# A spectral filter's transfers in 16-run pieces, and three loads begun later

## The chip, the cores and the metric

The kernel runs on one core of one Trainium2 chip. The metric is the time of one execution on the device in microseconds; several runs are given by their median. TensorE is called PE, VectorE DVE, ScalarE ACT, GpSimd POOL and SyncE SP. SP starts nearly all the transfers. The core has 16 DMA engines, which share all of them.

## The reference

Two blocks with residuals are computed forward and backward in bfloat16 over x of shape (1, 2048, 448): a spectral filter A and a token MLP B. The outputs are the result and the gradients to x, the filter's two parts, w1, b1, w2 and b2.

```python
def _A_ref(x, w_r, w_i):                      # x (1, 2048, 448); w_r, w_i (2048, 225)
    X = rfft2(x.astype(float32))
    X = X * (w_r + 1j * w_i)
    return irfft2(X, s=(S, D)).astype(bfloat16)

def _B_ref(x, w1, b1, w2, b2):                # w1 (2048, 1792), w2 (1792, 2048)
    h = layernorm(x)
    u = gelu(einsum("bsd,sf->bdf", h, w1) + b1)
    return (einsum("bdf,fs->bds", u, w2) + b2).transpose(0, 2, 1)

x = A_x
h  = x + _A_ref(layernorm(x), A_w_r, A_w_i)
h2 = h + _B_ref(layernorm(h), B_w1, B_b1, B_w2, B_b2)
# outputs: h2, and the vector-Jacobian product with grad_out for x, w_r, w_i, w1, b1, w2, b2
```

## The kernel before

The two-dimensional transform is done in steps of matmuls. `row_a` and `row_b` transform 16 row groups (the 448 axis and the first part of the 2048 axis), and after every second group a transfer on SP (line 667) puts the result into the buffer `D2` in another order of partitions, the D2 reshape. `s2_stage` then runs over four sets of groups: for each it does the second part of the 2048 axis with small matmuls on `D2` (line 223), multiplies with the filter (`fwd_mult` or `bwd_mult`), turns the product back with small matmuls, and sends it by SP (line 696) to the buffer `D3`, the D3 reshape. `inv_rows` does the inverse rows. Between these steps `fill(n)` gives PE n matmuls of an independent product from a list of pending generators: in the forward pass w2's product with grad_out (`dg_gen`, whose tiles `load_w2T` brings in by DMA transposes, line 306), in the backward pass the weight gradients out_6 and out_4 (`gw_gen`, operands by the transposes of lines 1166 and 1180, stores on lines 1275 and 1272).

PE, SP, DVE and ACT run their instructions in the order in which the kernel writes them, each engine in its own order; semaphores join them. A DMA is started by an instruction in SP's order, so an instruction of SP that takes long, or waits, keeps back all that was written after it. `defer` writes a transfer a little later, by an estimated PE clock. Matmuls go through line 218, DVE and ACT instructions through line 82.

The filter is kept in `W`, a view of region `rW`. `w_io` moves it between DRAM and `rW`: six moves for w_r and six for w_i, of which the generator gives one at each `next`. It loads w_r and w_i in the forward pass (row step t of the loop takes `W_AT[t]` moves) and stores their gradients, out_2 and out_3, in the tail (`gx_consumer` at step t takes as many moves as t occurs in `GW_AT`). The issue is line 572 in both cases. Of the six moves, the first brings the positive half of the frequencies: 64 rows of 7200 contiguous bytes, in DRAM as 4 x 16 rows. The four that follow bring the mirrored half, each 16 partitions in runs of 450 bytes (DF = 225 elements), and the last one 16 rows.

In the backward pass `load_du(q)` (line 1166) transposes a quarter of du for the second weight gradient, and `load_xall(q)` (line 1185) loads a quarter of x into region `rE` for the last LayerNorm's gradient. Quarter 3 of du is loaded in the du loop; quarters 0 and 2 inside `s2_stage`, which calls `after[s]()` when set s has been multiplied; quarter 1 in the last row steps, as are quarters 0 and 1 of x. Quarters 2 and 3 of x are loaded in the tail (`X_AT`).

In the tail, `gx_consumer` works on 8 slots of `r448`, and every second step stores two of them to out_1 (line 1340); eight steps later a slot is written again by DVE.

Of the kernel before, what the change touches and what calls it, by code (L numbers as in the profile page):

```python
# [17 lines left out]
P = 128  # L18
S = 2048
D = 448  # L20
DF = 225
# [18 lines left out]
N_FILL_B = (16, 16, 30, 8, 24, 8)  # L40
# [61 lines left out]
class Ring:  # L102
# [7 lines left out]
    def next(self):  # L110
        v = self.views[self.i % len(self.views)]
        self.i += 1
        Ring.release(v)
        return v
# [8 lines left out]
def kernel(  # L123
# [47 lines left out]
    def ring(reg, off, count, *dims):  # L171
        n = int(np.prod(dims))
        return Ring([cut(reg, off + i * n, *dims) for i in range(count)])

    def ps_ff(parts=P):
        return psum.tile([P, 512], F32, tag="ff", bufs=4, name="ps_ff")
# [5 lines left out]
    def evac(out, in_, scale=None):  # L182
        n = int(np.prod(in_.shape[1:]))
        if load[0] + sc.cost('copy', n, False) <= load[1] + ve.cost('tensor_copy', n, in_.dtype == BF16):
            if scale is None:
                sc.copy(out=out, in_=in_)
            else:
                sc.activation(out=out, in_=in_, func=ACT.Copy, scale=scale)
        elif scale is None:
            ve.tensor_copy(out=out, in_=in_)  # L190
        else:
            ve.tensor_scalar(out=out, in0=in_, scalar1=scale, scalar2=None, op0=ALU.mult)
# [5 lines left out]
    def run_due():  # L198
        while later and later[0][0] <= clock[0]:
            later.pop(0)[2]()  # L200

    def defer(us, fn, *views):
        state = [fn]

        def run():
            if state:
                state.pop()()
        later.append((clock[0] + us, len(later), run))
        later.sort(key=lambda x: x[0])
        for v in views:  # L210
            Ring.held.setdefault(id(v), []).append(run)

    def flush():
        while later:
            later.pop(0)[2]()
# [6 lines left out]
    def small(out, lhsT, rhs, start, stop):  # L222
        nc.tensor.matmul(out, lhsT=lhsT, rhs=rhs, start=start, stop=stop)  # L223
        clock[0] += int(np.prod(rhs.shape[1:])) / 38400.0

    def blk(i):
        return slice(32 * i, 32 * i + 32)
# [4 lines left out]
    def set_groups(s):  # L232
        return [8 * (s // 2) + s % 2 + 2 * a for a in range(4)]
# [154 lines left out]
    def newton_gp(v, y, sl):  # L388
        vi, yi = nt_i[:, 0, sl], y.bitcast(I32)
        a = nt_f[:, 0, sl]  # L390
        gp_.tensor_scalar(out=v, in0=v, scalar1=LN_EPS, scalar2=None, op0=ALU.add)
        gp_.tensor_scalar(out=yi, in0=v.bitcast(I32), scalar1=-0.5, scalar2=RSQRT_MAGIC, op0=ALU.mult, op1=ALU.add)
        for c0, c1 in RSQRT_STEPS:
            gp_.tensor_tensor(out=a, in0=y, in1=y, op=ALU.mult)
            gp_.tensor_tensor(out=a, in0=a, in1=v, op=ALU.mult)
            gp_.tensor_scalar(out=a, in0=a, scalar1=c0, scalar2=c1, op0=ALU.mult, op1=ALU.add)
            gp_.tensor_tensor(out=y, in0=a, in1=y, op=ALU.mult)
# [163 lines left out]
    def w_io(dr, di, store):  # L561
        Wq = Wc.rearrange("(q s) c g k -> s q c g k", s=2)
        for c_, d in ((0, dr), (1, di)):
            moves = [(Wq[0][:, c_].rearrange("q g k -> q (g k)"), 0, [[16 * DF, 4], [P * DF, 16], [1, 16 * DF]])]
            for i in range(4):
                g0 = 0 if i else 1
                moves.append((Wq[1][16 * i:16 * i + 16, c_, g0:NG, :], P - 16 * i - g0,
                              [[P * DF, 16], [-DF, NG - g0], [1, DF]]))
            moves.append((Wq[1][0:16, c_, 0, :], 64, [[P * DF, 16], [1, DF]]))
            for sb, row, dims in moves:  # L570
                d_ap = bass.AP(d.tensor, d.offset + row * DF, dims)
                nc.sync.dma_start(out=d_ap if store else sb, in_=sb if store else d_ap)  # L572
                yield
# [3 lines left out]
    X_ring = ring(rC, 0, 2, 4, 2, KW)  # L577
# [10 lines left out]
    def rowbase(s_):  # L588
        return 32 * (s_ // 4) + s_ % 4
# [80 lines left out]
    def s2_stage(get_x, on_mult, n1, n2, gap, after=None, scale=None):  # L670
        flush()

        def four(tables, s, turn, rhs):
            gs = set_groups(s)
            ps = [ps_ff()[:, 0:452].rearrange("p (c k) -> p c k", c=2) for _ in gs]
            for t, c, start, stop in ((tables[0], None, True, False), (tables[1], 0, False, False), (tables[2], 1, False, True)):
                for a, g in enumerate(gs):
                    for r in range(4):
                        x, o = rhs(a, g, r), ps[a][blk(r + turn * a & 3)]
                        small(o if c is None else o[:, c, :], lhsT=t[blk(r), g, :], rhs=x if c is None else x[:, 1 - c, :],  # L680
                              start=start, stop=stop)
            run_due()
            return ps

        y = None
        for s in range(5):
            if s < 4:
                x = get_x(s)
                for a, pv in enumerate(four((Vt, Ut, Un), s, 1, lambda a, g, r: D2[blk(r), g])):
                    evac(out=x[:, a], in_=pv, scale=scale)  # L690
            fill(n1)
            if s:
                for g, pv in zip(set_groups(s - 1), four((VTt, UTt, UTn), s - 1, -1, lambda a, g, r: y[blk(r), a])):
                    ab = r452_ring.next()
                    evac(out=ab, in_=pv)
                    defer(RESH_LAG, lambda g=g, ab=ab: resh[0].dma_start(out=D3[rowbase(g):rowbase(g) + 29:4, :, :, :], in_=ab), ab)
            if s < 4:
                y = Y_ring.next()
                for j in range(2):
                    on_mult(s, j, x[:, 2 * j:2 * j + 2], y[:, 2 * j:2 * j + 2])  # L700
            if after is not None and s in after:
                after[s]()
            fill(n2)
        fill(gap)
# [52 lines left out]
    def fill(n):  # L757
        while n > 0 and pending:
            try:
                next(pending[0])  # L760
                n -= 1
                if row_ops:
                    row_ops.pop(0)()
            except StopIteration:
                pending.pop(0)
# [75 lines left out]
    ve.reciprocal(out=rstd_x[:, 2:4], in_=rstd_x[:, 2:4])  # L841
    Rs.update({t: scale_R(t) for t in range(2, 4)})
    w_loads = w_io(A_w_r, A_w_i, False)
    uv = gen_UV()
    gen_inv_cols(0)
# [10 lines left out]
    GROUPS = {0: (6, 8), 1: (8, 10), 3: (10, 12), 5: (12, 14), 7: (14, 16)}  # L856
    STATS = {0: (6, 7), 1: (8, 9), **{t: (t + 8,) for t in range(2, 8)}}
    INV_S = {10: 0, 11: 1, 12: 2, 13: 3}
    W_AT = {t: 1 for t in range(1, 13)}
    for c in range(2):  # L860
        for e in range(2):
            sc.copy(out=Rp.rearrange("p (e a q b c) -> p c e a q b", e=2, c=2, q=8, a=2)[:, c, e],
# [3 lines left out]
    for t in range(NT):  # L866
# [21 lines left out]
        if t in GROUPS:  # L888
            a, b = GROUPS[t]
            newton_gp(mvx[:, a:b, 1], rstd_x[:, a:b], slice(a, b))  # L890
        for _ in range(W_AT.get(t, 0)):
            next(w_loads, None)
# [271 lines left out]
    def load_du(q):  # L1164
        n = du_t[q].shape[1] * 512
        nc.sync.dma_start_transpose(out=du_t[q].rearrange("p j b q -> p (j b) q"), in_=rD[:, 2048 * q:2048 * q + n])
# [10 lines left out]
    def st_load(n):  # L1177
        if n < 15:
            reg, j = order[n]
            nc.sync.dma_start_transpose(out=st_at[n], in_=reg[:, j * 1024 + 64:j * 1024 + 960])  # L1180
# [3 lines left out]
    def load_xall(q):  # L1184
        nc.sync.dma_start(out=xall[:, 4 * q:4 * q + 4, :], in_=x_pt[:, 4 * q:4 * q + 4, :])

    def rows(t):
        if t < NT:
            row_a(t, Rm[:])
            fill(2)  # L1190
        row_b(t - 4, True)
        fill(2 if t < NT else 1)
# [86 lines left out]
    for t in range(NT - LAG, NT + 4):  # L1279
        if t == 13:  # L1280
            st_load(3)
        if t == 14:
            load_xall(0)
        if t == 15:
            load_du(1)
        if t == 16:
            load_xall(1)
        if t == NT - 2:
            fill(8)
        rows(t)  # L1290
    fill(N_FILL_B[2])
    Meter.slack = 7.0
    s2_stage(lambda s: X_ring.next(), bwd_mult, 14, 22, N_FILL_B[4], {1: lambda: load_du(0), 3: lambda: load_du(2)},
             2.0 * INV_SD)
    Meter.slack = 2.0
    g_out = w_io(out_2, out_3, True)
    X_AT = {0: 2, 4: 3}
    GW_AT = tuple(range(12))

    def gx_consumer(t, py):  # L1300
        if t in X_AT:
            load_xall(X_AT[t])
        for _ in range(GW_AT.count(t)):
            next(g_out, None)
# [87 lines left out]
```

## Time and profile before

| | |
|---|---|
| Median of 3 runs | 370.64 us (367.15, 370.64, 371.81) |
| Profiled execution | 368.16 us, of which span 366.3 us |
| PE, DVE, ACT, POOL busy | 332.6, 251.1, 196.6, 64.0 us |
| DMA, mean over the span | 213 GB/s, 78.02 MB |
| Mean granted PE clock | 0.973 |

The span runs from the first to the last recorded instruction of one execution; the execution's own time is longer by what lies around it. Lines such as L572 are lines of the kernel. A row of a timeline gives start, length, engine, line, operation, output and inputs, count, and in brackets the idle time ahead of it with its releaser. SPq is SP's queue of DMA issues: its length is how long the issue held SP, not how long the data took. A row of windows gives, for each stretch, its length, the busy time of PE, PEld, DVE, ACT and POOL, then PE's granted clock, the mean busy share of the DMA engines and GB/s. The share can pass 1.00, because a packet's time is booked where its record stands and packets overlap.

### The profile page before, as it was taken

The numbers are of one execution on the slowest core, as the hardware profiler recorded it, in microseconds if no ns is written. First come the engines' busy times: TensorE is split into PE (matmuls) and PEld (weight loads), VectorE is DVE, ScalarE is ACT, GpSimd is POOL, SyncE is SP. The second block draws the span as 40 slices with busy tenths as digits, with TensorE's granted clock in tenths as the row PEclk, the third lists the DMA queues.
The fourth block names the chain that finished last, engine by engine and source line by source line (L and its number), as shares of the span: only waits on it lengthen the run. The fifth ranks groups of instructions, "written<-read, shape, count | busy, mean of one in ns | idle before, by whom it ended". The sixth has DMA issues, their size and how long they took to land.

```text
span 366.3 us, 7779 instructions
## 1 busy us (share of the span) xinstructions
PE 332.6 (91%) x2810; PEld 174.2 (48%) x2819; DVE 251.1 (69%) x666; ACT 196.6 (54%) x431; POOL 64.0 (17%) x219
## 2 busy tenths in 40 slices
PE   8679907989999999999999999999799999999694
PEld 3346604445654555555555555545333434555351
DVE  8896415781494788768224888786479984599594
ACT  5457512544696653622421345565368775679563
POOL 5766000000122000001000111110000000157361
PEclk9989977999999999999999999999999999999988
DMA  8999889767994999788776889839959699999784
GB/s 211 283 174 162 175 181 240 162 123 193 315 253 206 295 347 246 169 214 255 186 190 157 190 165 176 161 88 224 319 175 259 188 233 256 277 161 242 190 309 168
DMA packets 147006, 78.02 MB, mean 213 GB/s; under 512 B 95448, under 2 KB 139736, under 8 KB 146840
## 3 DMA queue, kind: packets, MB, share of 16 engines
q1 hardware_dynamic: 146680, 77.13, 85.6%
q8 instruction: 22, 0.36, 0.4%
q10 hardware_dynamic: 288, 0.39, 0.3%
q14 instruction: 16, 0.13, 0.1%
HBM read 25.71 MB, written 22.04 MB: 130 GB/s over the span
## 4 chain that ended last, share of the span: by engine, by line
PE 70%; DVE 9%; SPq 6%; DMA 6%; ACT 4%; issue 3%; POOL 0%; DVEq 0%; ACTq 0%
PE ps_mm L218 59%; PE ps_ff L218 7%; DVE r L82 5%; SPq L306 3%; PE ps_ff L223 3%; DVE rS L82 3%; DMA out_dram<-r 3%; ACT rO L82 2%; DMA rE<-in_A_x_dram 1%; DMA rA<-in_A_x_dram 1%; DVE rA L82 1%; SPq L667 1%; SPq L572 1%; DMA r<-rX 1%; SPq L316 1%
## 5 line engine op out<-in xcount | busy, mean ns | idle before, releaser
L218 PEld LDWEIGHTS <-r 128*128 128x128 bf16 (+2 forms) x600 | 56.3, 105 | 48.3 <-issue 5.7
L218 PEld LDWEIGHTS <-rS 128*128 128x128 bf16 (+2 forms) x496 | 40.3, 98 | 39.5 <-issue 6.6
L218 PE MATMUL ps_mm<-rD,r 128*128 128x448 bf16 x224 | 44.5, 352 | 0.0
L82 ACT CAST rO<-ps_mm 128x512 bf16<-128x512 f32 (+1 forms) x66 | 35.4, 583 | 14.5 <-PE ps_mm L218 10.4
L218 PEld LDWEIGHTS <-rst 128*128 128x128 bf16 (+1 forms) x320 | 23.6, 97 | 31.3 <-issue 14.4
L218 PE MATMUL ps_mm<-rC,rE 128*128 128x448 bf16 x144 | 33.1, 367 | 2.0 <-DMA rC<-in_grad_out_dram 1.9
L218 PE MATMUL ps_mm<-rB,r 128*128 128x448 bf16 x160 | 31.2, 352 | 0.1
L218 PE MATMUL ps_mm<-r,rst 128*128 128x512 bf16 (+2 forms) x144 | 28.1, 354 | 0.0
L218 PE MATMUL ps_mm<-rG,rst 128*128 128x512 bf16 (+1 forms) x122 | 26.7, 380 | 0.5 <-issue 0.3
L82 ACT CAST r<-ps_ff 128x452 bf16<-128x452 f32 x41 | 22.6, 588 | 8.3 <-PE ps_ff L223 6.0
L82 DVE SCALAR_TENSOR_TENSOR r<-ps_mm,b2col,r 128x448 bf16<-128x448 f32 x16 | 10.9, 683 | 19.9 <-PE ps_mm L218 17.0
L82 ACT ACTIVATE r<-ps_mm,rstd_h 128x448 bf16<-128x448 f32 x16 | 10.1, 633 | 26.8 <-PE ps_mm L218 26.8
L82 ACT ACTIVATE r<-rC 128x448 bf16<-128x448 bf16 x16 | 9.1, 571 | 26.6 <-DMA out_dram<-r 18.9
L218 PE MATMUL ps_mm<-rE,rS 128*128 128x448 bf16 x112 | 21.5, 352 | 0.0
L82 ACT ACTIVATE rG<-rG 128x896 bf16<-128x896 bf16 x14 | 13.3, 950 | 14.9 <-DVE rG L82 14.7
L218 PEld LDWEIGHTS <-rO 128*128 128x128 bf16 (+1 forms) x165 | 15.2, 98 | 12.3 <-ACT rO L82 0.2
L82 ACT CAST rS<-ps_ff 128x512 bf16<-128x512 f32 x31 | 17.9, 580 | 5.3 <-PE ps_ff L218 5.1
L82 ACT CAST rG<-ps_mm 128x512 bf16<-128x512 f32 (+1 forms) x33 | 16.5, 544 | 6.6 <-PE ps_mm L218 6.4
L218 PEld LDWEIGHTS <-rE 128*128 128x128 bf16 x144 | 13.8, 101 | 13.0 <-issue 4.0
L218 PE MATMUL ps_ff<-csI,rAT 113*128 113x224 bf16 (+1 forms) x108 | 19.4, 303 | 0.6 <-ACT rAT L82 0.4
L82 ACT CAST rAT<-ps_ff 113x512 bf16<-113x512 f32 x24 | 14.0, 591 | 10.7 <-PE ps_ff L218 10.6
L1134 POOL TENSOR_SCALAR lcol<-lcol 128x1 f32<-128x1 f32 x16 | 8.3, 519 | 64.9 <-ACT r L82 64.9
(189 smaller groups left out, 598.5 us busy)
## 6 DMA issues: line engine op xcount, KB each, us to landing
out_dram<-rO SPq DMA_DIRECT2D x34, 256.0 KB
r<-in_B_w_dram SPq DMA_DIRECT2D x5, 1024.0 KB
r<-r SPq DMA_DIRECT2D x32, 113.0 KB
rS<-in_B_w_dram SPq DMA_DIRECT2D x4, 896.0 KB
r<-r SPq DMA_DIRECT2D x12, 226.0 KB
out_dram<-rG SPq DMA_DIRECT2D x10, 256.0 KB
rO<-in_B_w_dram SPq DMA_DIRECT2D x2, 1024.0 KB
rC<-in_grad_out_dram SPq DMA_DIRECT2D x4, 448.0 KB
```

The costliest lines, as they stand in the source:

```text
L82: fn(**kw)
L218: nc.tensor.matmul(out, lhsT=lhsT, rhs=rhs, start=start, stop=stop)
L223: nc.tensor.matmul(out, lhsT=lhsT, rhs=rhs, start=start, stop=stop)
L306: nc.sync.dma_start_transpose(out=wT, in_=B_w2[j * P:(j + 1) * P, :].rearrange("f (t c) -> f t c", c=P))
L316: nc.sync.dma_start(out=go_tp[:, 4 * q:4 * q + 4, :], in_=go_tp_d[:, 4 * q:4 * q + 4, :])
L572: nc.sync.dma_start(out=d_ap if store else sb, in_=sb if store else d_ap)
L667: defer(RESH_LAG, lambda: resh[0].dma_start(out=D2[u:u + 125:4, 8 * e:8 * e + 8].rearrange("p g c k -> p (g c k)"), in_=cs.rearrange("p x ...
L1134: gp_.tensor_scalar(out=m1, in0=ms, scalar1=-1.0 / D, scalar2=None, op0=ALU.mult)
```

## The change

The filter's positive half is moved in four transfers of 16 rows instead of one of 64; each stands ahead of one of the four mirrored moves. So `w_io` gives 9 moves instead of 6 for each part. `W_AT` and `GW_AT` take two moves in odd steps, so that all 18 are still written by step 12 of the row loop, or step 11 of the tail. In the backward pass three transfers move out of the row steps into `s2_stage`: du's quarter 1 to after set 0, x's quarter 0 to after set 1 (behind du's quarter 0, which was there), and x's quarter 1 to after set 2.

```diff
     def w_io(dr, di, store):
         Wq = Wc.rearrange("(q s) c g k -> s q c g k", s=2)
         for c_, d in ((0, dr), (1, di)):
-            moves = [(Wq[0][:, c_].rearrange("q g k -> q (g k)"), 0, [[16 * DF, 4], [P * DF, 16], [1, 16 * DF]])]
+            moves = []
             for i in range(4):
+                moves.append((Wq[0][16 * i:16 * i + 16, c_].rearrange("l g k -> l (g k)"), 16 * i, [[P * DF, 16], [1, 16 * DF]]))
                 g0 = 0 if i else 1
                 moves.append((Wq[1][16 * i:16 * i + 16, c_, g0:NG, :], P - 16 * i - g0,
                               [[P * DF, 16], [-DF, NG - g0], [1, DF]]))
...
-    W_AT = {t: 1 for t in range(1, 13)}
+    W_AT = {t: 2 if t % 2 else 1 for t in range(1, 13)}
...
     for t in range(NT - LAG, NT + 4):
         if t == 13:
             st_load(3)
-        if t == 14:
-            load_xall(0)
-        if t == 15:
-            load_du(1)
-        if t == 16:
-            load_xall(1)
         if t == NT - 2:
             fill(8)
         rows(t)
     fill(N_FILL_B[2])
     Meter.slack = 7.0
-    s2_stage(lambda s: X_ring.next(), bwd_mult, 14, 22, N_FILL_B[4], {1: lambda: load_du(0), 3: lambda: load_du(2)},
+    s2_stage(lambda s: X_ring.next(), bwd_mult, 14, 22, N_FILL_B[4], {0: lambda: load_du(1), 1: lambda: (load_du(0), load_xall(0)), 2: lambda: load_xall(1), 3: lambda: load_du(2)},
              2.0 * INV_SD)
...
-    GW_AT = tuple(range(12))
+    GW_AT = tuple(range(12)) + tuple(range(1, 12, 2))
```

## Prediction

> **What bounds the kernel now.** I read the page first. TensorE (PE) is busy 91% of the span, so a gain can come only out of the places where PE stands.
>
> ```profile
> PE 332.6 (91%) x2810; PEld 174.2 (48%) x2819; DVE 251.1 (69%) x666; ACT 196.6 (54%) x431; POOL 64.0 (17%) x219
> ```
>
> PE's timeline has three gaps of more than a microsecond in the stretches that the change touches: 10.76 us before 57.11, 1.89 us before 260.59 and 3.27 us before 345.82. The bracket at the end of a row is the idle time and its releaser.
>
> ```profile
> 57.11 0.82 PE L223 MATMUL ps_ff<-r,Vt 32*32 32x452 bf16 x16 [10.76 <-DMA r<-rX]
> 260.59 0.41 PE L223 MATMUL ps_ff<-r,Vt 32*32 32x452 bf16 x16 [1.89 <-issue]
> 345.82 0.38 PE L218 MATMUL ps_ff<-RTm,r 128*113 128x128 bf16 x4 [3.27 <-DVE r L82]
> ```
>
> **Gap one** (forward). PE waits for the D2 reshape of rows 12 and 13 (L667). The rows were evacuated by 44.4, but their reshape is issued at 54.69. SyncE's timeline (SP; columns: start, length, line) says why: from 22.39 to 55.9 it issues back to back.
>
> ```profile
> 22.39 0.73 SPq L572 DMA_DIRECT2D rW<-in_A_w_r_dram  x1
> 23.16 7.10 SPq L306 DMA_TRANSPOSE rO<-in_B_w_dram  x1
> 30.31 0.71 SPq L572 DMA_DIRECT2D rW<-in_A_w_r_dram  x1
> 31.14 2.89 SPq L306 DMA_TRANSPOSE rE<-in_B_w_dram  x1
> ...
> 41.23 1.29 SPq L572 DMA_DIRECT2D rW<-in_A_w_i_dram  x2
> 42.62 6.59 SPq L306 DMA_TRANSPOSE rE<-in_B_w_dram  x1
> ```
>
> Four transposes of one size: two hold SP 2.89 and 3.07 us (the latter at 36.79, left out), two hold it 7.10 and 6.59. The two long ones stand behind the 64-run load of w_r and of w_i. The windows view gives the DMA rate (last column, GB/s) behind those loads, and behind the same two transfers as stores in the tail, beside an ordinary stretch each (30 to 42, 327 to 337):
>
> ```profile
> 24.00:30.00 6.00, 6.00 (x45) 3.95 (x44) 5.89 (x23) 4.42 (x10) 3.97 (x16) 0.86 0.94 93
> 30.00:42.00 12.00, 12.00 (x215) 8.06 (x214) 6.11 (x21) 7.91 (x16) 3.96 (x18) 1.00 1.02 187
> 320.00:326.00 6.00, 6.00 (x45) 2.98 (x44) 5.91 (x18) 4.47 (x12) 2.70 (x9) 1.00 1.05 113
> 327.00:337.00 10.00, 10.00 (x77) 5.67 (x74) 9.64 (x31) 9.02 (x26) 7.13 (x18) 1.00 1.10 284
> ```
>
> 93 and 113 GB/s where other transfers reach 187 and 284: the 64-run transfer runs on few DMA engines, and what is queued behind it waits.
>
> The Trainium skill, "DMA: Bandwidth & Descriptors", section "Why a DMA increments its semaphore by 16 and not by 1", says how many engines a copy gets: the largest number up to 16 that divides the slowest dimension of both sides. By it the old form (64 partitions against a DRAM pattern that begins with 4) gets 4 engines, the new one (16 against 16) gets 16. No row of before shows a 16-run copy of 7200 bytes, so that half of the rule is open.
>
> **Gap two** (start of the backward filter stage). Here too PE waits for a D2 reshape. SP's timeline before it holds the moved work:
>
> ```profile
> 248.43 0.52 SPq L1185 DMA_DIRECT2D rE<-in_A_x_dram  x1
> 249.04 0.54 SPq L667 DMA_DIRECT2D r<-r  x1
> 249.64 3.33 SPq L1166 DMA_TRANSPOSE rC<-rD  x1
> 253.01 1.05 SPq L1275 DMA_DIRECT2D out_dram<-rO  x2
> 254.17 0.39 SPq L1185 DMA_DIRECT2D rE<-in_A_x_dram  x1
> 254.61 1.63 SPq L667 DMA_DIRECT2D r<-r  x2
> ```
>
> **Gap three** (tail). The chain of waits shows an out_1 store that takes 9.86 us to land, issued right behind the 64-run store of w_i's gradient (333.96); VectorE (DVE) needs its buffer.
>
> ```profile
> 334.67 9.86 DMA out_dram<-r
> ...
> 344.65 1.13 DVE r L82 x3
> ```
>
> **The change, part by part.**
>
> *Forward loads.* Removed: the hold behind two 64-run loads. Against the mean of 2.89 and 3.07 (2.98) that is 7.10 - 2.98 + 6.59 - 2.98 = 7.73 us of SP time. Added: six issues on L572 (18 instead of 12). One took a median 0.607 us, the 64-run form 0.62 (at 315.52) like the 256-run forms, so I keep 0.61 plus a gap of 0.05: 6 x 0.66 = 3.96 us. All stand on SP ahead of the reshape that PE waits for, so both count in full: -7.73 + 3.96 = **-3.8 us**. The other steps do not get in the way: the ring slots of the transposes were free long before (the third weight tile's last matmul ran near 32 us), and the last rows were ready at 44.4, so SP stays the bound until 9.7 us are gained. Bounds: if the new runs' bytes are still paid by SP at the 229 GB/s of 49 to 55 us, each group holds 460.8 KB / 229 = 2.0 us and the gain is gone (-7.73 + 4.0 + 3.96 = +0.2). If a 16-run copy issues like the cheapest 128-run ones (0.39 at L1185), eight of them save 0.2 each, and with a hold 0.6 shorter the gain is 6.0. I take 3.8, because the transposes of 2.89 and 3.07 themselves stand right behind 112.5 KB transfers of L572, nearly the new size.
>
> A rule speaks against it. The row: on SP, transfers of 112.5 KB follow one another every 0.66 us, and from 49 to 55 us a queue of such pieces moves 229 GB/s. The Trainium skill, same page, "Bandwidth" and "Rules for kernel authors", wants 1 MiB per DMA and says that splitting over partitions only serializes; its SWDGE fit is 2.0 us plus bytes over 436 GB/s. By that, as an estimate, one copy of 460.8 KB is 3.1 us and four are 9.1, so the change would cost 6 us a group.
>
> *Moved loads.* x quarter 0 (0.52), the transpose of du's second quarter (3.33) and x quarter 1 (0.39) leave SP's queue ahead of the reshape: 4.24 us of issue and 0.92 MB of x. PE had other work until 258.70, and the evacuation that SP waited for (253.30) stays. Then the reshape goes out near 254.3; with the 2.28 us that the forward one took from issue to landing and 1.5 us for the 0.5 MB of stores ahead of it (about 340 GB/s around it) it lands at 258.1, before PE is free. **-1.9 us**, the whole gap; at least 1.0 if 0.9 of it stays. At their new place these three come after set 0, 1 and 2 of s2_stage. What queues behind them on SP: output stores of out_6 (L1275), weight tiles for later matmuls (L1180), and D3 reshapes (L696), needed at 312. The rO buffers of the stores are the tightest: six, one filled every 1.9 us, so 11.4 us round; less the 1.5 us of deferral and some 3.5 us to land, SP may be 6.4 us late before an evacuation stops. The transpose brings 1.8 to 3.3 (the four calls of L1166). Cost nothing, with that cover. The moved data is needed at 300.85 (rC) and at 317 (rE): some 35 us early.
>
> *Tail stores.* Again six issues more, but SP is not what the tail waits for: the 64-run stores held it (2.32 and 4.37 us at 318 and 320, where 0.6 and 1.5 are usual). The out_1 store of row 3 must land within 5.57 us (334.67 to 340.24). Less a hold of 3.6 to 4.1, 9.86 becomes 5.8 to 6.3, still 0.2 to 0.7 late; the store before (329.75) landed within 6.04 without stopping DVE, and a reshape lands in 2.28. From 340.24 DVE loses 4.42 us; PE loses 3.27 plus some 1.7 at the clock of 0.50 that the windows show from 347 to 350. Both are busy to the end after it, DVE being the tighter. **-4.4 us**, bounds 3.7 and 5.0.
>
> **Sum**: -3.8 - 1.9 - 4.4 = -10.1 us. PE works without a gap of more than a microsecond from 113 to 259, and loads there are released by its progress, so the first gain is carried. The profiled execution took 368.16 us (span 366.3 and 1.9 around it): 358.1. The median of three runs, 370.64, stands 2.5 above it, the lowest run 1.0 below; I go half way up: **359.3 us**.
>
> **The rivals.**
> - *The split only adds issues; it does not do what it says.* The waits view puts 3.8 us of the long transposes down to PE (L545), not to DMA; if the transposes were long by themselves, SP is 3.96 us later at gap one, gap three stays and gap two goes: 368.16 + 3.96 - 1.9 = 370.2, slower than before. It decides from where the relief per transpose is under 1.98 us. Against it: PE passed that tile's slot 10 us before, and both long ones stand behind the same form. 6%.
> - *The tail store is late anyway*, because ordinary stores fill the queues (284 GB/s from 327 to 337): 368.16 - 5.7 = 362.5. Against it: between 337 and 342 hardly half of that moved. 13%.
> - *The moved transfers hold the filter stage*: transpose 3.3 and x 0.92 MB at 340 GB/s, 2.7, make the out_6 stores over 6.4 us late and evacuations wait, as one did for 1.4 us near 257. 358.1 + 6.0 = 364.1. For it: SP issued back to back from 247 to 266. Against it: it stood idle later in set 0. 10%.
>
> **How the numbers follow.** Forecast 71%. Its bounds give gains from 4.5 (0.2 lost, 1.0, 3.7) to 12.9 (6.0, 1.9, 5.0), so 355.3 to 363.7 on the profiled time, 366.1 on the median: range 355 to 366, which takes in the second and third rival. A measurement of this kernel tells about 2% from no change; below 363.2 us it is faster by more. That holds for most of the forecast (0.68), about half of the second rival (0.07) and a corner of the third: 0.77. Within 2%: 0.18. Slower by over 2% needs the first rival with the tail's issues on the path: 0.05.
>
> **What would show it.** Right: all L306 transposes between 22 and 45 us near 3 us, with no stretch near 100 GB/s behind the L572 loads; PE's first gap near 7 us; no gap before the backward L223 group; no out_1 store over 6 us on the chain and no DVE wait on out_dram. Wrong: transposes of 6 us and more behind the new loads, a wait of ACT or DVE on out_dram<-rO within s2_stage, or a new PE gap there.

## The result and the profile after

The changed kernel takes 358.27 us, the median of four runs (357.57 to 359.34), against 370.6 us before: a ratio of 0.9684, 95% interval 0.9615 to 0.9754. Faster by 3.2%, 1 us under the forecast of 359.3. The profiled execution took 358.56 us, span 356.8. Ratios leave out executions more than 1.5% above the fastest of their kernel: eleven of the 25 of the kernel before (median 370.77 us) that stand beside the first four experiments, and in two experiments the profiled one (431 and 856 us), which the medians given for these two leave out too.

The page's line of busy time; PE's work is what it was, the span is 9.5 us shorter:

```profile
PE 331.0 (93%) x2810; PEld 173.6 (49%) x2819; DVE 251.1 (70%) x666; ACT 196.6 (55%) x431; POOL 63.6 (18%) x219
```

PE's timeline of the changed kernel at the three places of the forecast. The first gap is 6.89 us instead of 10.76; the other two rows have no bracket, so PE did not stand there at all:

```profile
53.49 0.82 PE L223 MATMUL ps_ff<-r,Vt 32*32 32x452 bf16 x16 [6.89 <-DMA r<-rX]
255.27 0.41 PE L223 MATMUL ps_ff<-r,Vt 32*32 32x452 bf16 x16
337.06 0.39 PE L218 MATMUL ps_ff<-RTm,r 128*113 128x128 bf16 x4
```

How far one and the same piece of PE's work moved shows where the time came from. A row_a group (before at 247.13, after at 243.77) starts 3.4 us earlier: the forward part. The gw_gen group at 272.70 is now at 267.38, 5.3 us earlier: another 2.0 from the start of the filter stage. The last matmuls (358.22, now 347.84) are 10.4 us earlier: another 5.1 in the tail. The span gained 9.5; what follows the last matmuls took 0.9 us more.

SP's timeline (start, length, line) where the two long transposes were; line numbers shift with the edits, 572 is 573 here:

```profile
22.73 1.37 SPq L573 DMA_DIRECT2D rW<-in_A_w_r_dram  x2
24.14 3.68 SPq L306 DMA_TRANSPOSE rO<-in_B_w_dram  x1
...
39.71 1.89 SPq L573 DMA_DIRECT2D rW<-in_A_w_i_dram  x3
41.70 2.52 SPq L306 DMA_TRANSPOSE rE<-in_B_w_dram  x1
```

7.10 and 6.59 us became 3.68 and 2.52, 7.5 us together; the filter's issues on SP are more by six. Windows rows (last column GB/s) behind the loads and, in the tail, in the stretch of the gradients' stores:

```profile
24.00:28.00 4.00, 3.99 (x26) 2.59 (x26) 3.97 (x17) 3.01 (x8) 2.18 (x11) 0.75 1.00 120
316.00:322.00 6.00, 6.00 (x51) 3.74 (x48) 5.94 (x20) 4.77 (x13) 3.58 (x11) 1.00 0.95 231
```

The tail's 113 GB/s became 231. Behind w_r's loads the rate rose only from 93 to 120, so the sign "no stretch near 100 GB/s" is met in part at best: there the shorter hold of the transpose tells the change, not the rate. And SP's queue ahead of the backward filter stage, without the moved transfers: the second of the two reshapes in the last row is the one that PE waited for before.

```profile
245.07 0.54 SPq L668 DMA_DIRECT2D r<-r  x1
245.70 1.04 SPq L1276 DMA_DIRECT2D out_dram<-rO  x2
246.84 2.13 SPq L668 DMA_DIRECT2D r<-r  x2
```

### The profile page after: what moved, and what is told of

Read it like the earlier page. It is cut to its first block, busy times and chain, and to the rows that moved or that the text cites. A ratio compares the mean times of both kernels' runs of the same rounds, so it can differ in the third digit from the quotient of the medians.

```text
span 356.8 us, 7788 instructions
## 1 busy us (share of the span) xinstructions
PE 331.0 (93%) x2810; PEld 173.6 (49%) x2819; DVE 251.1 (70%) x666; ACT 196.6 (55%) x431; POOL 63.6 (18%) x219
## 4 chain that ended last, share of the span: by engine, by line
PE 77%; DVE 7%; SPq 5%; ACT 4%; issue 2%; DMA 2%; DVEq 0%; POOL 0%; ACTq 0%
PE ps_mm L218 65%; PE ps_ff L218 8%; DVE r L82 4%; PE ps_ff L223 3%; SPq L306 3%; ACT rO L82 2%; DVE rS L82 2%; DMA rA<-in_A_x_dram 1%; SPq L573 1%; DVE rA L82 1%; DMA r<-rX 1%; ACT rX L82 1%; SPq L316 1%; SPq L668 1%; ACT rAT L82 0%
## 5 line engine op out<-in xcount | busy, mean ns | idle before, releaser
L218 PE MATMUL ps_mm<-r,rst 128*128 128x512 bf16 (+2 forms) x144 | 27.1, 345 | 0.0
L218 PEld LDWEIGHTS <-rO 128*128 128x128 bf16 (+1 forms) x165 | 15.2, 98 | 12.3 <-ACT rO L82 0.2
L1135 POOL TENSOR_SCALAR lcol<-lcol 128x1 f32<-128x1 f32 x16 | 8.5, 529 | 64.7 <-ACT r L82 64.7
L1308 POOL TENSOR_SCALAR lcol<-lcol 128x1 f32<-128x1 f32 x16 | 5.3, 332 | 75.9 <-ACT r L82 75.8
```

The lines of the kernel that those rows point to most:

```text
L1135: gp_.tensor_scalar(out=m1, in0=ms, scalar1=-1.0 / D, scalar2=None, op0=ALU.mult)
L1308: gp_.tensor_scalar(out=m1, in0=ms, scalar1=-2.0 / D, scalar2=None, op0=ALU.mult)
```

## Experiments

**One part alone, on the kernel before.** The first splits only the loads (code abridged).

```diff
-            moves = [(Wq[0][:, c_]..., 0, [[16 * DF, 4], [P * DF, 16], [1, 16 * DF]])]
+            moves = []
+            if store:
+                moves.append(...64 runs...)
             for i in range(4):
+                if not store:
+                    moves.append(...16 runs...)
...
-    W_AT = {t: 1 for t in range(1, 13)}
+    W_AT = {t: 2 if t % 2 else 1 for t in range(1, 13)}
```

> Only the loads of w_r and w_i are split into 16-run transfers; the gradients' stores keep the 64-run transfer, and no load is moved. Theory A (the 64-run transfer runs on four DMA engines and holds the transposes queued behind it): the L306 transposes behind the filter loads take about 3 us instead of 7.1 and 6.6, PE's first gap shrinks from 10.8 to about 7 us, the gaps of 1.9 and 3.3 us stay; 3.4 us less than before. Theory B (number and size of transfers count, not the engines): six more issues of 0.66 us ahead of the reshape, PE's first gap about 14.7 us, 4 us more than before.

Measured: 367.26 us, ratio 0.9923 (0.988 to 0.9966): 2.9 less by the ratio, 3.5 by the medians. The transposes take 3.34 and 2.82 us. PE's first gap, from its timeline:

```profile
53.53 0.82 PE L223 MATMUL ps_ff<-r,Vt 32*32 32x452 bf16 x16 [7.03 <-DMA r<-rX]
```

Theory A holds in its place, and theory B, that more issues can only cost, is out. But this profiled execution as a whole (368.3 us) was no shorter than the one before. One reason stands in the waits of the stretch from 240 to 275: DVE waited for a store of out_6, and PE was 27.35 us on the work from row_a to the gw_gen group that took 25.57 before and 23.61 in the changed kernel.

```profile
DVE rO L82 <- DMA out_dram<-rO: 2.0, 1, 2.0
```

The second splits only the stores (`if store:` in the same place, `GW_AT` as changed).

> Only the stores of the filter's gradients are split; loads and order of the moved transfers as before. Theory A: no out_1 store takes more than 6 us, PE's gap of 3.3 us and DVE's wait of 4.4 us in the tail are gone, the clock stays full there; 4.5 to 5 us less than before, nothing changed ahead of 310 us. Theory B: the tail has six more issues and the out_1 store is as late as before; 0 to 2 us more.

Measured: 365.87 us, ratio 0.9919 (0.9869 to 0.997): 3.0 less by the ratio, 4.9 by the medians, where theory A said 4.5 to 5. DVE's wait on out_dram<-r and PE's gap in the tail are gone from the profile, as theory A has it. But this execution's first gap was 14.14 us, with transposes of 8.38 and 7.59, although its forward part is the code of before. The third experiment, with the same forward part, had 12.43. So the 64-run load's hold is not a fixed price: 10.76 in the execution that the forecast was built on is the least of three.

The third moves only the three backward loads (the third part of the change's diff).

> Only the three backward loads are moved; the filter's transfers are the 64-run ones of before. Theory A: PE's gap of 1.9 us ahead of the backward L223 group is gone, both others stay; 1.9 us less than before. Rival (the moved transfers hold the filter stage or the tail): the gap is gone but DVE or ACT wait on rO stores later, 0 to 4 us more than before.

Measured: 369.1 us, ratio 0.9967 (0.9918 to 1.0015): inconclusive by its time, 1.2 less by the ratio and 1.7 by the medians. Its profile is clear: no gap ahead of the L223 group, the stretch from row_a to the gw_gen group 23.62 us, no wait on rO after it; the tail's gap of 3.35 stays. The rival of held-up evacuations is out.

**The engine count.** If it were only the size, two transfers of 32 runs would hold less than one of 64. (`W_AT` and `GW_AT`, left out here, write the two right behind each other.)

```diff
-            moves = [(Wq[0][:, c_]..., 0, [[16 * DF, 4], [P * DF, 16], [1, 16 * DF]])]
+            moves = [(Wq[0][32 * i:32 * i + 32, c_]..., 32 * i, [[16 * DF, 2], [P * DF, 16], [1, 16 * DF]]) for i in range(2)]
```

> The positive half in two transfers of 32 runs (DRAM pattern 2 x 16 rows) instead of one of 64, for loads and stores, the two next to each other; nothing else changed. Theory A, with the number of engines being what divides the slowest dimension of both sides: each runs on two engines, the same two, so the 450 KB go through two engines instead of four. The transposes behind take about 7.1 + 4.6 = 11 to 12 us, two more issues ahead of the reshape cost 1.3; PE's first gap about 20 us, the tail's gap longer by some 4 us; 10 to 15 us more than before. Theory B (smaller transfers hold less, each issue costs 0.66 us): the hold is the same or halved; between 3 us less and 1.5 us more than before.

Measured: 389.01 us, ratio 1.0518 (1.043 to 1.0607). SP's timeline, PE's first gap, and the windows row behind w_r's loads:

```profile
22.81 1.25 SPq L573 DMA_DIRECT2D rW<-in_A_w_r_dram  x2
24.10 11.80 SPq L306 DMA_TRANSPOSE rO<-in_B_w_dram  x1
...
49.21 11.31 SPq L306 DMA_TRANSPOSE rE<-in_B_w_dram  x1
```

```profile
68.35 0.81 PE L223 MATMUL ps_ff<-r,Vt 32*32 32x452 bf16 x16 [21.50 <-DMA r<-rX]
```

```profile
26.00:36.00 10.00, 9.80 (x126) 6.67 (x125) 7.32 (x28) 7.56 (x15) 6.88 (x28) 1.00 1.29 56
```

Halving the transfer made the hold longer: 11.80 and 11.31 us, where theory A said 11 to 12 and theory B no more than 7. The rate falls to 56 GB/s, from 93 with the 64-run form. The time is 18 us more, where theory A said 10 to 15: the tail grew more than expected, with a gap of 6.80 us and a second of 2.33. Number and size of transfers do not explain this.

The packet records of the traces, each with a start, a length and a size, show the engines at work. A run of 7200 bytes is one packet. Out_2's store before starts its packets four at a time every 0.27 us (at 318.37, 318.64 and 318.90 us); the two of 32 start them two at a time (at 330.93, 331.19 and 331.46), both transfers taken together, so both use the same two engines; the last piece of w_i in the changed kernel starts all its 16 within 0.06 us (at 49.54). That agrees with the rule on the number of engines (the Trainium skill, "DMA: Bandwidth & Descriptors", "Why a DMA increments its semaphore by 16 and not by 1"): four engines for a DRAM pattern that begins with 4, two for one that begins with 2, 16 for 16 rows. They also show what the hold is. Before, the last packets of the two 64-run loads end at 30.03 and 48.62, and the transposes behind them let SP go at 30.26 and 49.21; with two of 32 it is 35.56 and 59.96 against 35.90 and 60.52. Behind these loads SP is held until the slow copy is through.

**One part taken back, on the changed kernel (358.27 us).** The store of out_3 in one 64-run transfer again (code abridged):

```diff
+            if store and c_ == 1:
+                moves.append(...64 runs...)
...
-                moves.append(...16 runs...)
+                if not (store and c_ == 1):
+                    moves.append(...16 runs...)
...
-    GW_AT = tuple(range(12)) + tuple(range(1, 12, 2))
+    GW_AT = tuple(range(12)) + (1, 3, 5)
```

> The changed kernel, but the store of out_3 (w_i's gradient) has the 64-run transfer again. Theory A1 (the tail's gain is the one out_1 store that no longer lands behind the second 64-run store): DVE waits 3 to 5 us on an out_1 store of 8 us and more, PE has a gap of 2.5 to 4 us in the tail; about 363 us against 358.3 of the changed kernel. Rival A2 (the tail gains because SP is relieved in general, by both stores): about half, 360 to 361 us, and no single long out_1 store.

Measured: 359.58 us (358.46 to 361.14). Theory A1's stall did not come: DVE has no wait on an out_1 store, though the second one (L1338) stood right behind the 64-run store, as SP's timeline shows:

```profile
325.73 0.63 SPq L576 DMA_DIRECT2D out_dram<-rW  x1
326.47 0.70 SPq L1338 DMA_DIRECT2D out_dram<-r  x1
```

What differs is when. DVE's timeline has one row in the tail that can be found in these kernels, the short wait on ACT, before and here:

```profile
331.30 0.45 DVE L82 SCALAR_TENSOR_TENSOR r<-ps_ff,rstd_x,r 128x224 bf16<-128x224 f32 x1 [0.30 <-ACT r L82]
```

```profile
326.20 0.45 DVE L82 SCALAR_TENSOR_TENSOR r<-ps_ff,rstd_x,r 128x224 bf16<-128x224 f32 x1 [0.36 <-ACT r L82]
```

Against it the store is issued 3.4 us later before (334.67), 0.3 later here. DVE needs the buffer 8.9 us after that row, so the store has 5.6 us before and 8.7 here. The packet records show that half of A1 holds: the store landed late here too. Of its 128 packets 96 are through by 329.66; the other 32 run only from 333.20 to 334.94, at the end of and behind the packets of the 64-run copy (328.89 to 334.37). Before, these 32 run from 341.38 to 344.18, the copy's packets until 343.60. So the store took 8.5 us here, just inside its 8.7. Two of the four runs are above 360, which may be the cases in which 8.7 was not enough; no profile shows it.

That gave theory A3 and two more runs. Out_2's store alone in 64 runs (`c_ == 0`, `GW_AT` with 7, 9, 11):

> The changed kernel, but the store of out_2 (w_r's gradient) has the 64-run transfer again. With out_3 alone in 64 runs DVE did not stall in the profiled execution, though the out_1 store stood right behind it: that store had been issued 3 us earlier against DVE's work than in the kernel before. New theory A3 (the stall needs both: out_2's transfer makes SP late, out_3's then makes the late store land late): SP is held near 313 to 320 and issues the second out_1 store some 2 to 3 us later, but it lands in under 6 us and DVE waits less than 1 us; 358 to 359.5 us. Theory A2 (SP's relief alone): DVE waits 2 us or more; 360 or more.

Measured: 357.95 us (357.85 to 358.77). The chain of waits:

```profile
324.72 5.87 DMA out_dram<-r
...
330.71 0.83 DVE r L82 x3
```

SP is held again (a transpose on L1184 takes 4.22 us at 315.54), and the first two out_1 stores are issued 3.9 and 3.0 us later against DVE's row (325.54) than with both stores split. DVE waits 0.74 us for the first, which took 5.87 to land, and not for the second: theory A3, A2 is out. And both in 64 runs (`if not store`, `GW_AT` of before):

> The changed kernel with both gradient stores in 64-run transfers as before. Theory A3: DVE's wait of about 4.4 us and PE's gap of 3.3 us in the tail return; 362.5 to 363.5 us, more than the two single steps (about 1.3 for out_3 alone) add up to. If the steps simply add: 359.5 to 361.

Measured: 365.8 us (363.62, 365.76, 367.88), ratio 0.9874 (0.9786 to 0.9963) to the kernel before. The single steps cost -0.3 and +1.3, both together 7.5. By the times it needs both, as A3 says. No undisturbed profile shows the stall in this run; it stands in the three others that have both stores in 64 runs (DVE's longest wait on an out_1 store 4.42 before, 4.6 with the loads split, 4.3 with the loads moved). Why it is more than the 4.2 to 5.2 expected stays open.

The moved loads back in the row steps, everything else changed:

> The changed kernel with the three backward loads back in the row steps. If only PE's gap of 1.9 us ahead of the backward L223 group returns: 360.2 us. If evacuations also wait on late out_6 stores, as the runs with the loads in their old place showed (DVE 2.0 us before 254.49 in the run with split loads): up to 362 us. If the moves bring nothing: 358.3.

Measured: 362.1 us (362.06, 362.08, 363.76), 3.8 more than the changed kernel. By its time that is the case with late evacuations, not the 1.9 of the gap alone; no undisturbed profile shows them. Then only du's transpose back:

> The changed kernel with only the transpose of du's quarter 1 back in the row steps. If its 3.3 us on SP are what made the reshape and the out_6 stores late: PE waits ahead of the backward L223 group or on late evacuations, 360 to 362 us, most of what moving all three back cost (4.6 us). If the 0.9 MB of x were the greater part: under 359.5 us.

Measured: 357.96 us (357.3 to 359.17): it costs nothing. SP's timeline shows that without a quarter of x ahead of it the same transpose holds SP 1.88 us, not 3.33:

```profile
244.91 1.88 SPq L1167 DMA_TRANSPOSE rC<-rD  x1
```

So the loads of x are needed for the loss. Whether they alone cause all of it was not tried. What they may do besides lengthening the transpose, the chain of waits with the loads in their old place shows (here the run with split loads): the reshape behind x's quarter 1 took 5.33 us to land, where the forward one took 2.28.

```profile
251.96 5.33 DMA r<-r
```

**Is SP still the bound of the first gap?** One w2 transpose behind the reshapes (`CAP = 7`):

> The changed kernel with CAP 7 instead of 8: one of w2's transposes goes to SP after the last reshapes of the row loop instead of ahead of them. If SP's issue order is still what bounds PE's first gap (6.9 us in the changed kernel), the gap shrinks by that transpose's 2.5 to 2.9 us to about 4.2, and the time to 355.5 us. If the reshape is bound by its evacuation or its landing by now, nothing changes; if the transpose comes too late for the matmuls of its tile, PE gets a gap near 62 us and the time is 358 or more.

Measured: 356.77 us (356.69 to 357.74), ratio 0.962 (0.9587 to 0.9652) to the kernel before. By the medians it is the better version by some 1.5 us. The gap shrank by 1.4, about half of what was expected:

```profile
51.54 0.82 PE L223 MATMUL ps_ff<-r,Vt 32*32 32x452 bf16 x16 [5.48 <-DMA r<-rX]
```

Three w_i loads at 39.52 took 2.85 us on SP instead of 1.89; why is not shown. Then w_i's loads off SP altogether, first to GpSimd (`eng = nc.gpsimd if c_ and not store else nc.sync`):

> The changed kernel with w_i's nine loads issued by GpSimd instead of SP. If SP's issues are the bound, 9 x 0.66 = 5.9 us leave its queue ahead of the reshape and PE's first gap falls from 6.9 to about 1 to 2 us: 352.5 to 353.5 us. Rival: GpSimd's own issues are slow or start late, w_i lands after 55 us and fwd_mult waits for it; 357 us or more.

Measured: 361.16 us, the rival's side, but for another reason. GpSimd did not issue them in the row steps where the code writes them: its timeline has all nine at the start, beside the first loads of x. PE's row step 0 starts 8 us later than in the changed kernel (29.43 in PE's timeline, there 21.58):

```profile
2.40 5.47 POOL L574 DMA_DIRECT2D rW<-in_A_w_i_dram  x9
```

```profile
29.43 0.61 PE L218 MATMUL ps_ff<-rX,rS 128*128 128x128 bf16 x4 [6.53 <-DVE rX L82]
```

The gap that was aimed at did vanish (0.38 and 0.99 us are left). Then to ScalarE, which runs in the order of the code, with CAP 7:

> The changed kernel with CAP 7 and w_i's nine loads issued by ScalarE in the order of the code (row steps 7 to 12), not by SP. SP loses 5.9 us of issues ahead of the reshape: PE's first gap (5.5 us with CAP 7 alone) falls to 1 to 2.5 us, and the time to about 353 us, if ScalarE's evacuations have room (it is busy 6.9 of the 12 us from 34 to 46). Rival: the issues delay the evacuations of the row steps, which PE and the reshapes wait for; 355 to 359 us.

Measured: 356.63 us (355.43 to 358.08), the same as with CAP 7 alone and on the rival's side. Of the gap ahead of the L223 groups 0.37 and 0.99 us are left, but PE has gaps of 3.22 and 1.81 us in the row steps instead. Behind the second stands what ScalarE's timeline shows, two issues that took 5.75 us together and an evacuation that waited 5.35 us for them; the first follows an evacuation that waited 4.45 us, by the profile for a transpose of w2.

```profile
38.45 5.75 ACTq L574 DMA_DIRECT2D rW<-in_A_w_i_dram  x2
44.24 0.37 ACT L82 CAST UVT<-ps_ff 128x256 bf16<-128x256 f32 x1 [5.35 <-DMA rW<-in_A_w_i_dram]
```

The stall moved from one queue to another. That points to how fast the transfers drain as what holds the forward part from here on, rather than to who issues them; no run separates the two.

## Why the prediction was right, point by point

**Forward loads, 3.8 forecast.** 3.6 measured between the profiled executions, 3.4 of it kept to 243. The mechanism held, as the packet records show, and so did the terms: 7.5 us of hold saved for 7.73, six issues more, and the new runs held no more than others of their size. Of the two lines of evidence one was weaker than it looked: a rate of 93 GB/s beside 187 in the forward part, where the changed kernel still has 120. The lower bound, that SP still pays for the bytes, did not come. Against the median the term was probably under-sized: the 64-run loads' gap was 10.76, 12.43 and 14.14 us in three executions, the split ones' 6.89, 7.03, 7.26, 7.37 and 6.89 in five, which makes the mean gain at this gap 12.4 - 7.1 = 5.3. (The run with the loads alone kept only 2.9 to 3.5 of it.) This may be part of the 2.5 us between the profile and the median of before; I had gone half way up for want of a reason, so that the forecast came within 1 us was partly luck. The runs' spread fits: 365.79 to 374.8 in 25 before, 357.57 to 359.34 in four after.

**Moved loads, 1.9 forecast.** 2.0 measured between the profiled executions, for the right event (the reshape goes out earlier) but the wrong part: I put 3.33 of the 4.24 us down to the transpose, and the run with the transpose back shows that alone it costs nothing. The chain of waits before ran over x's quarter 1, 5.11 us from its issue at 254.17, and my working gave x's data no price of its own. And the cover that I priced for the new place was thin in the old one: evacuations waited for out_6 stores and the stretch was 27.4 us in two executions instead of 25.57, which fits the 3.8 that the moves were worth in the changed kernel.

**Tail stores, 4.4 forecast, bounds 3.7 to 5.0.** 5.1 measured, just above the upper bound. The step said: the out_1 store lands late because it stands behind the second 64-run store. That holds, as its last 32 packets show. But it was half of the cause: alone it costs DVE nothing in the profiled execution. It takes the first 64-run store as well, which made the out_1 store's issue some 3 us later. I had seen the hold at 318 and 320 and called it harmless, because SP was not what the tail waited for at that moment. The change split both stores, so the omission did no harm; that was luck. The landing was mis-sized too: I left the store 5.8 to 6.3 us, 0.2 to 0.7 late, and in the changed kernel its packets are through 2.3 us after its issue (327.34 to 329.63). So the whole wait of 4.42 went; DVE's next wait on ACT, 0.75 us before (352.01) and 0.30 now (341.70), is part of the rest.

**The end** had no term: from PE's last matmuls to the end of the span it took 0.9 us more. Why was not tried.

**The rivals.** That the split only adds issues is refuted by the run with the loads alone, and once more by the two of 32. The tail store late anyway: no out_1 store is on the changed kernel's chain. The filter stage held: no wait on rO stores in it. The rule against splitting, with its 6 us a group, did not hold here: the run with the loads alone has its first gap shorter by 3.7 us, not longer by 12.

## What to carry to other kernels

When a transfer is followed by a long issue, look at how many of its packets start at a time before its size: here a copy whose DRAM pattern began with 4 or 2 ran on four or two DMA engines, and what stood behind it in SP's queue waited for these; four pieces on all engines cost less than one piece on four, and two pieces on two engines cost most. A stall with a tight deadline can need two causes, one that makes the issue late and one that makes the landing long, so undo each alone and both together. If several profiles of one piece of code differ, the one that you price from may be the best of them.

## What the runs showed that was not expected

- The hold of one and the same 64-run load differs by execution: transposes of 7.10 and 6.59, 7.50 and 7.58, 8.38 and 7.59 us. The copies' own packets take 6.1 and 6.0, 6.4 and 7.0, 7.4 and 6.7 us from first to last, where 16 rounds of 0.27 us would be 4.3.
- With a quarter of x (448 KB) ahead of it the transpose of du's quarter 1 held SP 3.33, 3.41 and 3.49 us in three executions, 1.88 without. It is not the only thing that does so: the changed kernel has one of 3.07 us at 289.48 with no load of x right ahead of it.
- ScalarE's own queue backs up like SP's: two loads took 5.75 us to issue there, and ScalarE's next instruction waited 5.35 us for them.
- The parts measured alone on the kernel before (2.9, 3.0 and an unclear 1.2 us by the ratios; 3.5, 4.9 and 1.7 by the medians) do not add up to the whole's 11.7 by the ratio and 12.3 by the medians. They fall short by 4.6 and 2.2 us. The stretches in the profiles may explain a part (holds that vary, evacuations that wait on one another); the rest stays open.
